# Hash attention and an MLP mixer on one core: wide hash products for the first pair, a new cadence of weight conversion, and an early fetch of the second turned batch

## The chip, the cores and the metric

The kernel runs on one core of one Trainium2 chip. The metric is the time of one execution on the device in microseconds (us), as the median of some runs. A run's time is about 1.8 us longer than the span of its instructions in the trace, so spans and times are not mixed below: a figure is called a span where it is one.

## The reference, cut to what matters

```python
# attention: batch 4, heads 8, sequence 768, head size 64, six hash bits
q_bits = (np.einsum('bhsd,dk->bhsk', q, proj) > 0)      # k_bits alike
mask = q_bucket[:, :, :, None] == k_bucket[:, :, None, :]
scores = np.where(mask, scale * q @ k^T, -1e9)
attn = softmax(scores);  x = attn @ v                   # -> (B, S, 512)
# mixer, weights in float64
h = relu(x^T @ w_tok1) @ w_tok2                         # token mixing
u = x + h^T
out = u + relu(u @ w_ch1) @ w_ch2                       # channel mixing
```

The kernel has three stages: attention for 16 pairs of heads (each in two halves of 384 queries), token mixing for four batches, and channel mixing. The weights come as float64; the chip turns each piece of 128x768 into float32 with five VectorE operations, a square on ScalarE, and a sixth VectorE operation. Below, such a piece is a *conversion*, and its three steps are *begin*, *join* and *end*. Attention leaves its result as XT, channels on partitions; token mixing wants batches 0 and 1 (and 2 and 3) *turned*, so XT goes out to memory in a *bounce* and comes back with *fetch*.

## The kernel before

The hash of a pair is four 32-wide products side by side. VectorE makes plus or minus a half of them, and a transfer brings the bits into the rows where they act as six extra channels of the score product (a seventh row carries a constant). For the first pair, nothing hides that transfer.

```python
def hashes(n):
    g = pool.tile([P, HALF], BF16, name="g", tag="g", bufs=2)
    ps = psum.tile([P, 2, 512], F32, name="hp", tag="sc", bufs=3)[:, 0]   # a bank of the scores
    for j in range(4):
        nc.tensor.matmul(ps[32 * j : 32 * j + 32, :HALF], projblk, loaded[n][0][:, j % 2, sl], ...)
    for rows in [slice(0, 64), slice(64, P)] if n == 0 else [slice(0, P)]:
        nc.vector.tensor_scalar(g[rows], ps[rows, :HALF], 0.0, 0.5, op0=ALU.is_gt, op1=ALU.subtract)
        ...                                     # n == 0: scaled on VectorE
    if n:
        nc.scalar.mul(g, g, bitscale)           # later pairs: scaled on ScalarE
    ...                                         # eight transfers g -> bit rows
```

One half of attention, in program order. `weights.some` does one third of a conversion in each half, so the square falls now into first, now into second halves:

```python
now = Half(n, half)
now.scores()                      # six chunks: product, bits' product, exponential
if half == 0: add_values(n)
now.add(0)
... quotients.sums()              # first halves: sums of the pair before
if half == 0 and n + 1 < len(pairs):
    hashes(n + 1); load_qk(n + 2)
if quotients: quotients.newton()  # three VectorE operations, four copies on ScalarE
if half and n and n % 2 == 0: bounce(pool, n - 2)
now.add(1)
if n:
    weights.some(third); third = (third + 1) % 3
if before: before.weigh()         # 12 products (24 records in a trace), then num on ScalarE
```

The end of attention and the start of token mixing:

```python
    before.weigh()
    quotients.divide()
    bounce(pool, len(pairs) - 2)  # last bounce: waits for VectorE's transposes
# token mixing
    fetch(1, x1)                  # same queue, behind it
    jobs = jobs(weights(pool))    # first loads of weights, behind that
    # jobs: three conversions of w_ch1 (two pieces), two jobs of weight sums, eight conversions of w_ch2;
    # mix1 and mix2 do one job after each of their parts
    for b in range(B):
        mix1(b)
        if b: mix2(b - 1)
    mix2(B - 1)
```

Of the kernel before, what the change touches and what calls it, by code (L numbers as in the profile page):

```python
# [36 lines left out]
F32 = mybir.dt.float32  # L37
# [11 lines left out]
def kernel(  # L49
# [40 lines left out]

    ident = const.tile([P, P], F32, name="ident")
    make_identity(nc, ident)
    ones = const.tile([P, D], F32, name="ones")
    nc.vector.memset(ones, 1.0)

    projblk = const.tile([P, 32], F32, name="projblk")
    nc.scalar.dma_start(out=projblk, in_=proj_pair)


    bitscale = const.tile([P, 1], F32, name="bitscale")  # L100
    nc.gpsimd.memset(bitscale, BIG)
    for j in range(4):
        if j % 2 == 0:
            nc.gpsimd.memset(bitscale[32 * j : 32 * j + 32], 1.0)
        else:
            for i in range(2):
                nc.gpsimd.affine_select(
                    out=bitscale, in_=bitscale, compare_op=ALU.not_equal, fill=-NB * BIG,
                    base=-(32 * j + 16 * i + NB), pattern=[[0, 1]], channel_multiplier=1,
                )  # L110
    largest = const.tile([P, B * NP], F32, name="largest")
# [14 lines left out]
    class Conversion:  # L126
# [72 lines left out]

        def some(self, k):  # L200

            (self.begin, self.join, self.end)[k]()
            if k == 0:
                self.fetch()

# [46 lines left out]
    def attention(pool, psum, W1, W2, x0):  # L252
        zeroed = [pool.tile([P, 2, S], BF16, name=f"bits{n}", tag=f"bits{n}", bufs=1) for n in range(2)]
        loaded = {}

        def load_qk(n):
            if n >= len(pairs):
                return
            b, hp = pairs[n]
            t = pool.tile([P, 2, S], F32, name="qk", tag="qk", bufs=3)  # L260
            for sl in [slice(0, HALF), slice(HALF, S)] if n == 0 else [slice(0, S)]:
                nc.sync.dma_start(out=t[:, :, sl], in_=qk[b, hp, :, :, sl])
            loaded[n] = [t, None, None, None]
# [18 lines left out]
        def hashes(n):  # L282

            g = pool.tile([P, HALF], BF16, name="g", tag="g", bufs=2)
            ps = psum.tile([P, 2, 512], F32, name="hp", tag="sc", bufs=3)[:, 0]
            for j in range(4):
                sl = slice(HALF * (j // 2), HALF * (j // 2) + HALF)
                nc.tensor.matmul(  # L288
                    ps[32 * j : 32 * j + 32, :HALF], projblk, loaded[n][0][:, j % 2, sl],
                    start=True, stop=True,  # L290
                )
            for rows in [slice(0, 64), slice(64, P)] if n == 0 else [slice(0, P)]:
                nc.vector.tensor_scalar(
                    g[rows], ps[rows, :HALF], 0.0, 0.5, op0=ALU.is_gt, op1=ALU.subtract,
                )
                if n == 0:
                    nc.vector.tensor_scalar(g[rows], g[rows], bitscale[rows], None, op0=ALU.mult)
            if n:
                nc.scalar.mul(g, g, bitscale)
            for j in range(4):  # L300
                sl = slice(HALF * (j // 2), HALF * (j // 2) + HALF)
                for i in range(2):
                    at = 32 * j + 16 * i
                    issuer = nc.scalar if n == 0 and i else nc.sync
                    issuer.dma_start(
                        out=zeroed[n % 2][D * i : D * i + NB + 1, j % 2, sl], in_=g[at : at + NB + 1],
                    )

        class Half:
# [5 lines left out]
            def scores(self):  # L315

                qkt, bits = loaded[self.n][0], zeroed[self.n % 2]
                qs = slice(HALF * self.half, HALF * self.half + HALF)
# [10 lines left out]
                def exponential(sc):  # L329
                    e = pool.tile([P, 2, HALF], F32, name="e", tag="e", bufs=12)  # L330
                    nc.scalar.activation(e, sc[:, :, :HALF], ACT.Exp, scale=SCALE)  # L331
                    self.es.append(e)

                waiting = []
                for c in range(NR):
                    sc = psum.tile([P, 2, 512], F32, name="sc", tag="sc", bufs=3)
                    product(sc, qkt, c, True)
                    if first and c < GR:
                        waiting.append((c, sc))
                        if c == GR - 1:  # L340
                            for c, sc in waiting:
                                product(sc, bits, c, False)
                            for c, sc in waiting:
                                exponential(sc)
                        continue
                    product(sc, bits, c, False)
                    exponential(sc)

            def add(self, k):
# [28 lines left out]
        class Quotients:  # L378
# [34 lines left out]
            def divide(self):  # L413
# [4 lines left out]
                )  # L418


        nc.scalar.preload_act_table_set("natural_log_exp_and_others")
        load_qk(0)
        for t in zeroed:
            nc.gpsimd.memset(t, 0.0)
        load_qk(1)

        idle = psum.tile([P, 512], F32, name="idle", tag="sm", bufs=1)
        for _ in range(14):
            nc.tensor.matmul(idle[:D, :D], ones, ones, start=True, stop=True)
        hashes(0)  # L430
        load_v(0)
        weights = Conversion(
            pool,
            [(w_tok1, W1, 3, (0, NR)), (w_tok2, W2, 1, (0, NJ)), (w_ch1, WC1, 1, (0, NCB - 1))],
            bufs=2,
        )
        before, both = None, []
        third = 0
        for n in range(len(pairs)):
            for half in range(2):  # L440
# [17 lines left out]
                now.add(1)  # L458
                if n:
                    weights.some(third)  # L460
                    third = (third + 1) % 3
                if before:
# [7 lines left out]
                before = now  # L470
        while third or weights.fetched:
            weights.some(third)
            third = (third + 1) % 3
        quotients = Quotients(both)
# [3 lines left out]
        quotients.divide()  # L478
        bounce(pool, len(pairs) - 2)

# [87 lines left out]
    def tokens(pool, psum, W1, W2, x0, weights, jobs, T):  # L568
# [7 lines left out]
        if not turned:  # L576
            fetch(1, x1)
        jobs = jobs(weights(pool)) if jobs else []

        def job():  # L580
            if jobs:
                jobs.pop(0)()
# [50 lines left out]
        mix2(B - 1)  # L633
        while jobs:
            job()
# [195 lines left out]
    def attention_and_tokens(W1, W2, x0):  # L831
# [7 lines left out]
        def weights(pool):  # L839
            return Conversion(  # L840
                pool, [(w_ch1, WC1, 1, (NCB - 1, NCB)), (w_ch2, WC2, 3, (0, NHT))], bufs=3,
            )

        def jobs(conversion):
            n1, n2 = DCH // NW, NHT * DM // NW
            return [
                *[conversion.one] * (n1 + 1),
                *weight_sums(
                    WC1, SW1, slice(0, NCB // 2), slice(NCB // 2, NCB),
                    slice(0, DCH // 2), slice(DCH // 2, DCH),  # L850
                ),
                *[conversion.one] * n2,
            ]
# [65 lines left out]
```

## Time and profile before

| What | Before |
|---|---|
| Median of the runs | 861.52 us (3 runs, 861.51 to 861.9) |
| The profiled run | 860.13 us, span 858.3 us, mean clock of TensorE 0.992 |
| TensorE busy | 842.5 us, 98% |

The stretches of the stages, from the profile of the kernel before. The columns are the stretch, its length, then busy time and number of instructions of TensorE, its weight loads, VectorE, ScalarE and GpSimd, TensorE's granted clock, the share of the transfer engines and GB/s. The stretches are attention from the first weighing, the last sums and weighing, and token mixing:

```profile
22.49:320.57 298.08, 298.08 (x2059) 136.87 (x2057) 246.05 (x300) 231.76 (x356) 0.00 (x0) 1.00 0.39 127
320.57:326.07 5.50, 5.50 (x34) 1.92 (x32) 3.11 (x5) 3.13 (x6) 0.00 (x0) 1.00 0.00 0
326.07:420.07 94.00, 87.27 (x225) 44.16 (x224) 74.91 (x100) 14.79 (x20) 0.00 (x0) 0.95 0.44 151
```

Of these three stretches, only token mixing has TensorE idle (94.00 against 87.27 us) and under a lower clock (0.95). Attention shows a full TensorE.

### The profile page before, as it was taken

Reading aid. Unit: us, or ns where it says so; the run is one execution under the profiler, and the core shown is the slowest. Engines: PE = TensorE matmul, PEld = TensorE weight load, DVE = VectorE, ACT = ScalarE, POOL = GpSimd, SP = SyncE. Lnnn points to the kernel's source line nnn. Section 1 sums busy time; section 2 is a strip of 40 time slices with the busy share of each in tenths; the row PEclk is TensorE's granted clock in tenths of the full one; section 3 lists DMA queues with packets and bytes.
Section 4 is the critical chain, followed back from the end, with each engine's and each line's share of the span. In section 5 each row is a group of like instructions: output and inputs, shape, how many; then the busy total and the mean of one; then the engine's idle time right before and its main releaser. Section 6 shows DMA issues by size and latency. Waiting matters only on the chain.

```text
span 858.3 us, 9068 instructions
## 1 busy us (share of the span) xinstructions
PE 842.5 (98%) x3449; PEld 386.3 (45%) x3449; DVE 530.8 (62%) x650; ACT 316.8 (37%) x492; POOL 52.8 (6%) x51
## 2 busy tenths in 40 slices
PE   8999999999999998999999999999999999999997
PEld 4444444444444443554544444444444444444444
DVE  3788878788888882999565383624467332336411
ACT  4777778778778772122011101011210101111000
POOL 1000000000000000000001112001110201011110
PEclk9999999999999999999999999999999999999999
DMA  4235353362534315632102101312210120000001
GB/s 151 88 145 173 105 166 114 113 204 97 150 113 129 134 38 188 234 129 75 37 0 74 73 1 61 112 72 73 74 37 29 36 94 13 0 0 1 24 25 52
DMA packets 48866, 73.72 MB, mean 86 GB/s; under 512 B 27952, under 2 KB 29616, under 8 KB 48816
## 3 DMA queue, kind: packets, MB, share of 16 engines
q1 hardware_dynamic: 48472, 72.90, 25.0%
q8 instruction: 29, 0.48, 0.2%
q14 instruction: 21, 0.17, 0.1%
q10 hardware_dynamic: 344, 0.17, 0.1%
HBM read 59.79 MB, written 12.58 MB: 84 GB/s over the span
## 4 chain that ended last, share of the span: by engine, by line
PE 88%; DVE 8%; DMA 2%; issue 1%; ACT 0%; SPq 0%; DVEq 0%; ACTq 0%
PE b L673 50%; PE sc L324 19%; PE acc L366 15%; PE sums L390 2%; PE t L617 1%; PE hp L288 1%; DVE tmp L184 1%; DVE tmp L168 1%; DMA raw<-in_moe_w_ch 1%; DVE XT L623 1%; DVE WC L195 1%; DVE tmp L180 1%; DVE tmp L165 1%; DVE tmp L185 1%; DMA qk<-in_qk 1%
## 5 line engine op out<-in xcount | busy, mean ns | idle before, releaser
L324 PE MATMUL sc<-qk 64*128 64x384 f32 x768 | 160.5, 497 | 1.0 <-ACT e L331 0.7
L331 ACT ACTIVATE e<-sc 128x768 f32<-128x768 f32 x192 | 151.3, 813 | 17.6 <-PE sc L324 17.1
L680 ACT COPY p<-b 128x512 f32<-128x512 f32 x72 | 42.3, 587 | 302.6 <-PE b L673 302.6
L366 PE MATMUL acc<-e,vn 128*64 128x384 f32 x768 | 130.9, 490 | 0.0
L358 DVE TENSOR_TENSOR esd<-esd,e 128x768 f32<-128x768 f32 x128 | 122.3, 955 | 10.0
L673 PE MATMUL b<-r,WC 128*128 128x512 f32 (+1 forms) x300 | 125.6, 575 | 0.0
L673 PE MATMUL b<-T,SW 128*128 128x512 f32 x216 | 96.6, 592 | 0.0
L324 PEld LDWEIGHTS sc<-qk 64*128 64x128 f32 x768 | 66.7, 188 | 58.3 <-issue 43.8
L673 PEld LDWEIGHTS b<-r,WC 128*128 128x128 f32 x300 | 57.0, 190 | 67.1 <-issue 63.6
L366 PEld LDWEIGHTS acc<-e,vn 128*64 128x64 f32 x768 | 52.3, 137 | 74.9 <-issue 74.9
L673 PE MATMUL b<-T,WC 128*128 128x512 f32 x144 | 67.7, 592 | 0.0
L703 DVE TENSOR_TENSOR r<-p,u 128x512 f32<-128x512 f32 x18 | 12.5, 693 | 86.5 <-ACT u L680 86.5
L673 PE MATMUL b<-XT,WC 128*128 128x512 f32 x144 | 64.7, 592 | 0.0
L324 PE MATMUL sc<-bits 64*128 64x384 bf16 x384 | 63.4, 324 | 1.3 <-DMA bits<-g 1.3
L673 PEld LDWEIGHTS b<-T,SW 128*128 128x128 f32 x216 | 41.0, 190 | 51.7 <-issue 50.9
L699 POOL TENSOR_TENSOR p<-p,p 128x512 f32<-128x512 f32 x18 | 22.8, 1264 | 652.2 <-ACT p L680 641.5
L673 PE MATMUL b<-r,SW 128*128 128x512 f32 x144 | 62.8, 592 | 0.0
L598 PE MATMUL t<-x,W 128*128 128x512 f32 x96 | 45.1, 629 | 3.8 <-DMA x<-bounced 3.8
L617 PE MATMUL t<-W,r 128*128 128x384 f32 x128 | 43.5, 499 | 2.9 <-DVE XT L623 2.9
L354 DVE SCALAR_TENSOR_TENSOR esd<-e 128x768 f32<-128x768 f32 x32 | 30.6, 956 | 21.8 <-ACT e L331 21.6
L680 ACT COPY u<-b 128x512 f32<-128x512 f32 x24 | 14.1, 587 | 79.1 <-PE b L673 79.1
L673 PEld LDWEIGHTS b<-T,WC 128*128 128x128 f32 x144 | 27.4, 190 | 34.4 <-issue 34.4
(79 smaller groups left out, 737.2 us busy)
## 6 DMA issues: line engine op xcount, KB each, us to landing
raw<-in_moe_w_ch SPq DMA_DIRECT2D x16, 768.0 KB
seen<-in_qk SPq DMA_DIRECT2D x16, 768.0 KB
qk<-in_qk SPq DMA_DIRECT2D x15, 768.0 KB
vn<-in_v SPq DMA_DIRECT2D x16, 384.0 KB
vt<-in_vT SPq DMA_DIRECT2D x16, 384.0 KB
bounced<-stage SPq DMA_DIRECT2D x32, 192.0 KB
x<-bounced SPq DMA_DIRECT2D x4, 1536.0 KB
out<-p SPq DMA_DIRECT2D x18, 256.0 KB
```

Of the source, the lines that this page charges most:

```text
L324: nc.tensor.matmul(sc[:, i, :HALF], t[rows, 1, P * c : P * c + P], t[rows, 0, qs], start=start, stop=not start,)
L331: nc.scalar.activation(e, sc[:, :, :HALF], ACT.Exp, scale=SCALE)
L354: nc.vector.scalar_tensor_tensor(self.d, es[0], NR * EPS, es[1], op0=ALU.add, op1=ALU.add,)
L358: nc.vector.tensor_tensor(self.d, self.d, e, op=ALU.add)
L366: nc.tensor.matmul(acc[D * i : D * i + D], vn[:, i, c], e[:, i], start=(c == 0), stop=(c == NR - 1),)
L390: nc.tensor.matmul(ps[at : at + 32], ones[:, :32], self.halves[h].d[:, i], start=True, stop=True,)
L598: nc.tensor.matmul(ps, W1[:, r, P * j : P * j + P], x[:, r], start=(r == 0), stop=(r == NR - 1),)
L617: nc.tensor.matmul(ps[:, :HALF], r1[:, j, P * cb : P * cb + P], W2[:, j, HALF * half : HALF * half + HALF], start=(j == 0), stop=(j == NJ ...
L673: nc.tensor.matmul(self.ps[i][:, cols], left(k), right(k)[:, cols], start=first and k == ks[0], stop=k == ks[-1], skip_group_check=True,)
L680: nc.scalar.copy(c, self.ps[i])
L699: nc.gpsimd.tensor_tensor(p7, p5, p7, op=ALU.add)
L703: nc.vector.tensor_tensor(r[:, 3], p7, u, op=ALU.add)
```

## The change

It has three parts. *Start:* the first pair's bits come from four 128-wide products whose result already stands in the right rows, so VectorE writes the bits and no transfer is needed. The first key/query load is split over two queues. *Cadence:* second halves do end, fetch and begin of a conversion, first halves the join; so twelve conversions fit into attention where ten did, and the last block of the first channel weight is among them. *Fetch:* the fetch of the second turned batch and the first loads of weights go ahead of the last bounce. The diff, cut to its core:

```diff
+        def turnover(self):
+            self.end()
+            self.fetch()
+            self.begin()
 ...
+                issuer = nc.scalar if n == 0 and sl.start else nc.sync
+                issuer.dma_start(out=t[:, :, sl], in_=qk[b, hp, :, :, sl])
 ...
+        def first_hashes(which, half):
+            sl = slice(HALF * half, HALF * half + HALF)
+            ps = psum.tile([P, 512], F32, name="hw", tag="sm" if which else "acc", bufs=1)[:, :HALF]
+            nc.tensor.matmul(ps, projwide, loaded[0][0][:, which, sl], start=True, stop=True)
+            to = bitrows[0][:, which, sl]
+            nc.vector.tensor_scalar(to, ps, 0.0, 0.5, op0=ALU.is_gt, op1=ALU.subtract)
+            if which:
+                nc.vector.tensor_scalar(to, to, widescale, None, op0=ALU.mult)
 ...                                          # in the first half's scores():
+                if first:
+                    first_hashes(0, 0)
+                    first_hashes(1, 0)
                 for c in range(NR):
 ...
                         if c == GR - 1:
+                            first_hashes(1, 1)
                             for c, sc in waiting:
                                 product(sc, bits, c, False)
 ...
+                if first:
+                    first_hashes(0, 1)
 ...
-        hashes(0)
-            [(w_tok1, W1, 3, (0, NR)), (w_tok2, W2, 1, (0, NJ)), (w_ch1, WC1, 1, (0, NCB - 1))],
+            [(w_tok1, W1, 3, (0, NR)), (w_tok2, W2, 1, (0, NJ)), (w_ch1, WC1, 1, (0, NCB))],
 ...
-                if n:
-                    weights.some(third)
-                    third = (third + 1) % 3
+                if half:
+                    weights.turnover()
+                else:
+                    weights.join()
 ...
         quotients.divide()
-        bounce(pool, len(pairs) - 2)
 ...
             fetch(1, x1)
-        jobs = jobs(weights(pool)) if jobs else []
+            jobs = jobs(weights(pool))
+            bounce(pool, len(pairs) - 2)
```

More of the change, by code (lines that the diff above doesn't have):

```diff
@@ L88, with cancel @@
     const = ctx.enter_context(tc.tile_pool(name="const", bufs=1))
-    ident = const.tile([P, P], F32, name="ident")
-    make_identity(nc, ident)
+    projs = const.tile([P, P + 32], F32, name="projs")
+    nc.scalar.dma_start(out=projs, in_=proj_pair)
+    projwide, projblk = projs[:, :P], projs[:, P:]
     ones = const.tile([P, D], F32, name="ones")
     nc.vector.memset(ones, 1.0)
-    projblk = const.tile([P, 32], F32, name="projblk")
-    nc.scalar.dma_start(out=projblk, in_=proj_pair)
+    def cancel(scale, at):
+        nc.gpsimd.affine_select(
+            out=scale, in_=scale, compare_op=ALU.not_equal, fill=-NB * BIG,
+            base=-at, pattern=[[0, 1]], channel_multiplier=1,
+        )
+    widescale = const.tile([P, 1], F32, name="widescale")
+    nc.gpsimd.memset(widescale, 0.0)
+    for i in range(2):
+        nc.gpsimd.memset(widescale[D * i : D * i + NB], BIG)
+        cancel(widescale, D * i + NB)
     bitscale = const.tile([P, 1], F32, name="bitscale")
@@ L106 @@
             for i in range(2):
-                nc.gpsimd.affine_select(
-                    out=bitscale, in_=bitscale, compare_op=ALU.not_equal, fill=-NB * BIG,
-                    base=-(32 * j + 16 * i + NB), pattern=[[0, 1]], channel_multiplier=1,
-                )
+                cancel(bitscale, 32 * j + 16 * i + NB)
+    ident = const.tile([P, P], F32, name="ident")
+    make_identity(nc, ident)
     largest = const.tile([P, B * NP], F32, name="largest")
@@ L198, in end @@
             )
-        def some(self, k):
-            (self.begin, self.join, self.end)[k]()
-            if k == 0:
-                self.fetch()
+        def turnover(self):
+            self.end()
+            self.fetch()
+            self.begin()
         def one(self):
@@ L252, in attention @@
     def attention(pool, psum, W1, W2, x0):
-        zeroed = [pool.tile([P, 2, S], BF16, name=f"bits{n}", tag=f"bits{n}", bufs=1) for n in range(2)]
+        bitrows = [pool.tile([P, 2, S], BF16, name=f"bits{n}", tag=f"bits{n}", bufs=1) for n in range(2)]
         loaded = {}
@@ L261, in load_qk @@
             for sl in [slice(0, HALF), slice(HALF, S)] if n == 0 else [slice(0, S)]:
-                nc.sync.dma_start(out=t[:, :, sl], in_=qk[b, hp, :, :, sl])
+                issuer = nc.scalar if n == 0 and sl.start else nc.sync
+                issuer.dma_start(out=t[:, :, sl], in_=qk[b, hp, :, :, sl])
             loaded[n] = [t, None, None, None]
@@ L291, in hashes @@
                 )
-            for rows in [slice(0, 64), slice(64, P)] if n == 0 else [slice(0, P)]:
-                nc.vector.tensor_scalar(
-                    g[rows], ps[rows, :HALF], 0.0, 0.5, op0=ALU.is_gt, op1=ALU.subtract,
-                )
-                if n == 0:
-                    nc.vector.tensor_scalar(g[rows], g[rows], bitscale[rows], None, op0=ALU.mult)
-            if n:
-                nc.scalar.mul(g, g, bitscale)
+            nc.vector.tensor_scalar(g, ps[:, :HALF], 0.0, 0.5, op0=ALU.is_gt, op1=ALU.subtract)
+            nc.scalar.mul(g, g, bitscale)
             for j in range(4):
@@ L303, in hashes @@
                     at = 32 * j + 16 * i
-                    issuer = nc.scalar if n == 0 and i else nc.sync
-                    issuer.dma_start(
-                        out=zeroed[n % 2][D * i : D * i + NB + 1, j % 2, sl], in_=g[at : at + NB + 1],
-                    )
+                    nc.sync.dma_start(
+                        out=bitrows[n % 2][D * i : D * i + NB + 1, j % 2, sl], in_=g[at : at + NB + 1],
+                    )
+        def first_hashes(which, half):
[6 more added lines that the diff above has]
+                nc.vector.tensor_scalar(to, to, widescale, None, op0=ALU.mult)
         class Half:
@@ L315, in scores @@
             def scores(self):
-                qkt, bits = loaded[self.n][0], zeroed[self.n % 2]
+                qkt, bits = loaded[self.n][0], bitrows[self.n % 2]
                 qs = slice(HALF * self.half, HALF * self.half + HALF)
@@ L418, in divide @@
                 )
+        load_qk(0)
         nc.scalar.preload_act_table_set("natural_log_exp_and_others")
-        load_qk(0)
-        for t in zeroed:
-            nc.gpsimd.memset(t, 0.0)
+        nc.gpsimd.memset(bitrows[1], 0.0)
         load_qk(1)
@@ L437, in attention @@
         before, both = None, []
-        third = 0
         for n in range(len(pairs)):
@@ L458, in attention @@
                 now.add(1)
-                if n:
-                    weights.some(third)
-                    third = (third + 1) % 3
+                if half:
+                    weights.turnover()
+                else:
+                    weights.join()
                 if before:
@@ L470, in attention @@
                 before = now
-        while third or weights.fetched:
-            weights.some(third)
-            third = (third + 1) % 3
+        assert not (weights.fetched or weights.begun or weights.ready)
         quotients = Quotients(both)
@@ L577, in tokens @@
             fetch(1, x1)
-        jobs = jobs(weights(pool)) if jobs else []
+            jobs = jobs(weights(pool))
+            bounce(pool, len(pairs) - 2)
         def job():
-            if jobs:
+            if not turned and jobs:
                 jobs.pop(0)()
@@ L633, in tokens @@
         mix2(B - 1)
-        while jobs:
+        while not turned and jobs:
             job()
@@ L839, in weights @@
         def weights(pool):
-            return Conversion(
-                pool, [(w_ch1, WC1, 1, (NCB - 1, NCB)), (w_ch2, WC2, 3, (0, NHT))], bufs=3,
-            )
+            return Conversion(pool, [(w_ch2, WC2, 3, (0, NHT))], bufs=3)
         def jobs(conversion):
-            n1, n2 = DCH // NW, NHT * DM // NW
             return [
-                *[conversion.one] * (n1 + 1),
                 *weight_sums(
@@ L851, in jobs @@
                 ),
-                *[conversion.one] * n2,
+                *[conversion.one] * (NHT * DM // NW + 1),
             ]
@@ L898 @@
         "in_proj": np.ascontiguousarray(inputs["proj"]),
-        "in_proj_pair": np.zeros((2 * D, 32), np.float32),
+        "in_proj_pair": np.zeros((2 * D, 2 * D + 32), np.float32),
     }
@@ L902 @@
         proj = inputs["proj"]
-        arrays["in_proj_pair"][D * i : D * i + D, 16 * i : 16 * i + proj.shape[1]] = proj
+        for at in (D * i, 2 * D + 16 * i):
+            arrays["in_proj_pair"][D * i : D * i + D, at : at + proj.shape[1]] = proj
     for name in _WEIGHTS:
```

## The prediction

> **What bounds the kernel now.** I read the page first, then the waits of TensorE, then the chain, then the timeline around each hole. On the page, line 1 is busy time by engine and the second line heads the chain that ended last:
>
> ```profile
> PE 842.5 (98%) x3449; PEld 386.3 (45%) x3449; DVE 530.8 (62%) x650; ACT 316.8 (37%) x492; POOL 52.8 (6%) x51
> ...
> PE 88%; DVE 8%; DMA 2%; issue 1%; ACT 0%; SPq 0%; DVEq 0%; ACTq 0%
> ```
>
> TensorE is the bound, so time can be won only where it is idle or runs slowly. The waits of TensorE (total, count, longest) list the holes:
>
> ```profile
> PE t L598 <- DMA x<-bounced: 3.8, 1, 3.8
> PE t L617 <- DVE XT L623: 2.9, 1, 2.9
> PE sc L324 <- DMA bits<-g: 1.3, 1, 1.3
> ```
>
> The timeline (start, length, engine) shows what each hole costs in all, by groups of the same work:
>
> ```profile
> 326.07 10.57 PE L598 MATMUL t<-x,W 128*128 128x512 f32 x24
> 329.95 2.18 SPq L232 DMA_DIRECT2D bounced<-stage  x4
> 332.24 0.58 SPq L239 DMA_DIRECT2D x<-bounced  x1
> 340.46 13.61 PE L598 MATMUL t<-x,W 128*128 128x512 f32 x24 [3.82 <-DMA x<-bounced]
> 374.52 10.48 PE L617 MATMUL t<-W,r 128*128 128x384 f32 x32
> 407.07 0.95 DVE L195 SCALAR_TENSOR_TENSOR WC<-raw,tmp 128x768 f32<-128x768 f32 x1
> 408.54 12.02 PE L617 MATMUL t<-W,r 128*128 128x384 f32 x32 [2.92 <-DVE XT L623]
> ```
>
> Hole 1: the second batch (x) is asked for at 332.24, because SyncE's queue stands behind four writes that wait for VectorE's transposes. Its product starts at 340.46 after 3.82 us idle, then takes 13.61 us where the same 24 records took 10.57. Hole 2: VectorE is still converting weights (L195) when it should empty PSUM (L623); 2.92 us idle, then 12.02 in place of 10.48.
>
> At the start, the chain and the timeline show the hash bits:
>
> ```profile
> 8.99 1.85 DMA bits<-g
> 11.77 0.82 ACT e L331
> ...
> 18.33 0.61 ACT L299 ACTIVATE g<-g,bitscale 128x384 bf16<-128x384 bf16 x1
> 18.84 4.60 ACT L331 ACTIVATE e<-sc 128x768 f32<-128x768 f32 x6
> 22.49 4.09 PE L366 MATMUL acc<-e,vn 128*64 128x384 f32 x24
> ```
>
> The first scores wait for a bounce through DMA until 10.97 and the first exponential runs at 11.77. But note L299 at 18.33: ScalarE scales the second pair's bits ahead of the second half's exponentials. A small loss repeats in attention, shown by two half-stages of equal work and what ScalarE did in the longer one:
>
> ```profile
> 46.14 5.05 PE sc L324 x36
> 56.64 5.28 PE sc L324 x36
> ...
> 57.11 0.91 ACT L194 ACTIVATE raw<-raw 128x768 f32<-128x768 f32 x1
> 58.37 4.43 ACT L331 ACTIVATE e<-sc 128x768 f32<-128x768 f32 x6
> ```
>
> **What the Trainium skill says.** (1) "TensorE: Matmul & The Clock Gate", Part 1: an idle window of about 3.4 us halves the clock until a busy window has passed. The trace agrees: weight loads follow each other every 0.86 us after hole 1 and every 0.43 us before it. (2) Same page, Part 3: products with few output columns run side by side in column tiles. Agrees: four 32-wide hash products take 0.65 us together in the chain, as one full-width product of 384 columns does (L617: 10.32/16 = 0.645). (3) Same page, "Architectural detail": ScalarE and VectorE are strict FIFO. Nothing in this trace contradicts it; my start estimate rests on it. (4) "DMA: Bandwidth & Descriptors", "Issuing engines are not separate DMA queues": transfers from different queues share the 16 engines and interleave. This trace has no large pair at once to show it.
>
> **The change, part by part.**
>
> *Fetch of the second batch.* Now issued before the last bounce, so SyncE no longer waits for the transposes at 329.95. Its buffer may still wait for TensorE's last use of the memory, at the latest the end of attention at 326.0. Before, issue to start of the product took 340.46 - 332.24 = 8.2 us, so the data is there by 334.3 at the latest, ahead of 336.6 when it is wanted. Removed: 3.82 idle and 13.61 - 10.47 = 3.14 of slow clock, **6.96 us**.
>
> *First channel weight converted in attention.* VectorE's token stage had 10 conversions and has 8. One conversion is 0.60+0.99+0.60+0.99+0.96+0.87 = 5.0 us by its starts in the timeline, and the first need no longer wait for weights landing at 342.5. In before's clock, VectorE does transposes to 329.95, the weight sums (four of 1.7) to 336.9, two conversions to 346.0, and the emptying of the first mix2 from 348 to 359, with a conversion between. By the built order the last heavy conversion then ends near 388, and the emptying of the third mix2, whose first bank is full near 389, is prompt. Mix2 of the last batch (starting 398) finds free banks. Removed: 2.92 + (12.02 - 10.48), **4.46 us**. Check of both: with no hole the stage is 4 x (10.30 + 10.32) = 82.5 us where it took 420.07 - 326.07 = 94.0; difference 11.5.
>
> *Attention's cadence.* A conversion per 2 halves in place of 3. Does VectorE still fit? In the pair from 124.86 to 144.42 (19.56 us), which has a bounce, a join and an end, VectorE idled 0.25 + 0.76 + 0.59 = 1.60 us. The change adds a begin, 0.60 + 0.99 = 1.59 us: it just fits. It makes the adds of the next half 1.3 us later, which the two waits for the hash and for the reciprocal swallow; sums wait for nothing new. So hidden. Two gains follow. The square (L194) now always stands in second halves, away from the reciprocal copies, so the five halves of 5.28 become 5.05: 5 x 0.23 = **1.2 us**. And the last pair has no conversion (join, 2.5 us before its adds), so the last sums, 1.52 in the chain where others take 0.78, no longer wait: **0.7 us**.
>
> *Start.* Removed: the bits' transfers (1.85) and two of four small VectorE steps. Added: four full-width products of 0.64 in place of 0.65 together, so 1.9 us more TensorE work. The queue half-and-half load lets the key/query halves and the next pair share the engines; I take the first half at TensorE at 5.1 in place of 4.64 (an estimate; the next transfer is 0.39 MB beside it). Two products, partly at the slow clock, to 6.7; three scores of 0.65 to 8.6; third product 9.25; first exponential near **9.6**, 2.2 earlier. But that gain doesn't reach the second half. The fourth product follows the sixth score chunk, which waits for the third exponential: 9.6 + 2.4 + 0.1 + 0.8 + 0.64 = 13.55. VectorE has its bits (0.56) ahead of the three adds (3.0) and then the next pair's hash (0.6); ScalarE's L299 (0.6) waits for that, and the next six exponentials stand behind it in FIFO: 13.55 + 0.2 + 0.56 + 3.0 + 0.6 + 0.6 = **18.5**, where before it was 18.84. TensorE meanwhile has three chunks to do (to 16.7) and idles till 19.4. If the clock stays fast, weighing starts 0.6 earlier than 22.49; if the 2.7 us hole drops the clock, 1.1 later. About evens: **0.2 us lost**, give or take 1.2.
>
> Sum: 6.96 + 4.46 + 1.2 + 0.7 - 0.2 = 13.1, so 861.5 - 13.1 = **848.4 us**.
>
> **The rivals.** *A: the start gains fully*, 2 to 2.5 us, 846. For: the first exponential really is earlier. Against: VectorE and ScalarE orders as built. *B: VectorE becomes attention's bound.* Its margin on a pair with a bounce is 0.01 us by the above; 0.3 us short on each of five such pairs would give 850, and spread over twelve pairs 852. Against: pairs without a bounce have 1.8 us to spare, so a lag should not add up. *C: hole 2 stays*, since one conversion more (5 us) stands between TensorE's banks and their emptying at mix2(1): 852 to 853. Against: eight banks and a lead of over 10 us by my walk through the order. *D: the fetch is held* by memory still in use or by sharing with the two weight loads behind it (0.79 MB each beside 1.57 MB): a remnant of hole 1 of 1 to 3 us, 850 to 851. Before, such loads also stood right behind it.
>
> **Range and chances.** The token stage is firm to about 0.7 us, attention to about 1, the start to about 1.5; together some 2, with a tail to the slow side from B to D. 845.8 to 851.0 holds 8 in 10. Faster by over 2% needs 844.3, 4 us better than the sum: even rival A in full falls short. Slower by over 2% has no mechanism.
>
> **What would show it.** In the changed profile: no wait for x and none for XT L641 (L623 before) among TensorE's waits; mix1 of the second batch about 10.5 long right after the first; the sc groups all 5.05; sums last 0.8; first exponential near 9.6 but the second half's six near 18.5, behind a g scale, with a hole in TensorE of some 2.7 us before it. Wrong if the second half's exponentials start near 16, if sc or acc groups of the first twelve pairs stretch, or if a new wait stands in the token stage.

## The result, and the profile after

The changed kernel took **846.46 us** (median of 4 runs, 845.84 to 846.74) where the kernel before took 861.51 us in the same comparison (4 runs, 859.83 to 861.9). The ratio is 0.983, with an interval of 0.981 to 0.985: 1.7% less time, within 2%. Ratios here are the mean time of one kernel's fast runs over that of the other's fast runs of the same rounds, so they are not quite the ratio of the quoted medians.

Lines were added above most of the code, so a line number moves: the scores L324 are now L340, weighing L366 is L388, the sums L390 are L412, the products of token mixing L598 and L617 are L616 and L635, and the emptying L623 is L641. From the page of the changed kernel, busy time by engine and the head of the chain:

```profile
PE 835.2 (99%) x3449; PEld 384.8 (46%) x3449; DVE 532.3 (63%) x652; ACT 318.7 (38%) x492; POOL 52.0 (6%) x55
...
PE 98%; DVE 1%; DMA 0%; ACT 0%; issue 0%; DVEq 0%; ACTq 0%
```

TensorE's share of the chain went from 88% to 98%, VectorE's from 8% to 1%. TensorE's waits in the changed kernel:

```profile
PE sc L340 <- DVE g L305: 1.5, 1, 1.5
...
PE sc L340 <- ACT e L347: 0.9, 2, 0.6
PE hw L319 <- DMA qk<-in_qk: 0.8, 1, 0.8
```

Both large waits of token mixing are gone, and one new wait of 1.5 us on the hash g stands at the head. The same three stretches as before, in the changed kernel:

```profile
22.24:319.13 296.89, 296.89 (x2058) 137.17 (x2057) 256.95 (x314) 235.92 (x358) 0.00 (x0) 1.00 0.43 136
319.13:323.93 4.80, 4.80 (x34) 1.79 (x32) 1.58 (x3) 3.12 (x6) 0.00 (x0) 1.00 0.87 330
323.93:406.52 82.59, 82.59 (x227) 42.67 (x226) 66.17 (x88) 12.88 (x18) 0.00 (x0) 1.00 0.39 124
```

Token mixing has TensorE busy all of its 82.59 us at a full clock. Subtracting stage by stage gives the account of the whole gain in the traces:

| Stage | Before | After | Gain | Predicted |
|---|---|---|---|---|
| Start, to the first weighing | 22.49 | 22.24 | 0.25 | -0.2 |
| Attention | 298.08 | 296.89 | 1.19 | 1.2 |
| Last sums and weighing | 5.50 | 4.80 | 0.70 | 0.7 |
| Token mixing | 94.00 | 82.59 | 11.41 | 11.42 |
| Channel mixing | 438.23 | 438.28 | -0.05 | 0 |
| Span | 858.30 | 844.80 | 13.50 | 13.1 |

In the timeline of the changed kernel (start, length, engine) the fetch is issued before the last weighing ends, mix1 of the first and second batch run as one group, and the four bounce writes stand behind:

```profile
315.21 0.38 SPq L251 DMA_DIRECT2D x<-bounced  x1
...
323.93 20.87 PE L616 MATMUL t<-x,W 128*128 128x512 f32 x48
...
327.81 3.16 SPq L244 DMA_DIRECT2D bounced<-stage  x4
```

In its chain a score group, and the last sums that took 1.52 us before:

```profile
36.83 5.05 PE sc L340 x36
...
319.20 0.78 PE sums L412 x8
```

In the chain all groups of 36 score records are 5.04 or 5.05, except the very last half's 5.15. At the start, from the timeline (the number in brackets is the idle time before, and what ended it):

```profile
9.70 4.43 ACT L347 ACTIVATE e<-sc 128x768 f32<-128x768 f32 x6 [6.58 <-PE sc L340]
...
17.60 0.55 DVE L305 TENSOR_SCALAR g<-hp 128x384 bf16<-128x384 f32 x1
...
18.21 0.92 PE L340 MATMUL sc<-qk 64*128 64x384 f32 x4 [1.51 <-DVE g L305]
18.25 0.62 ACT L306 ACTIVATE g<-g,bitscale 128x384 bf16<-128x384 bf16 x1 [3.30 <-DVE g L305]
18.77 4.41 ACT L347 ACTIVATE e<-sc 128x768 f32<-128x768 f32 x6
```

The first exponential is 2 us earlier than before, the second half's are where they were: 18.77 against 18.84. This is the one place where the change gains nothing of what it could.

### The profile page after: what moved, and what is told of

It reads as the page before. It is cut to its first block, busy times and chain, and to the rows that moved or that the text cites. A ratio compares the mean times of both kernels' runs of the same rounds, so it can differ in the third digit from the quotient of the medians.

```text
span 844.8 us, 9068 instructions
## 1 busy us (share of the span) xinstructions
PE 835.2 (99%) x3449; PEld 384.8 (46%) x3449; DVE 532.3 (63%) x652; ACT 318.7 (38%) x492; POOL 52.0 (6%) x55
## 4 chain that ended last, share of the span: by engine, by line
PE 98%; DVE 1%; DMA 0%; ACT 0%; issue 0%; DVEq 0%; ACTq 0%
PE b L691 51%; PE sc L340 19%; PE acc L388 15%; PE t L616 5%; PE t L635 5%; PE sums L412 1%; PE hp L301 1%; DMA qk<-in_qk 0%; PE hw L319 0%; DVE esd L380 0%; ACT e L347 0%; DVE esd L376 0%; ACT g L306 0%; DVE bits L321 0%; DVE u L777 0%
## 5 line engine op out<-in xcount | busy, mean ns | idle before, releaser
L340 PE MATMUL sc<-qk 64*128 64x384 f32 x768 | 158.6, 492 | 2.4 <-DVE g L305 1.5
L347 ACT ACTIVATE e<-sc 128x768 f32<-128x768 f32 x192 | 152.9, 812 | 14.0 <-PE sc L340 13.2
L388 PE MATMUL acc<-e,vn 128*64 128x384 f32 x768 | 130.9, 490 | 0.0
L380 DVE TENSOR_TENSOR esd<-esd,e 128x768 f32<-128x768 f32 x128 | 122.3, 955 | 10.3 <-ACT e L347 0.5
L340 PEld LDWEIGHTS sc<-qk 64*128 64x128 f32 x768 | 66.5, 187 | 58.1 <-issue 44.9
L388 PEld LDWEIGHTS acc<-e,vn 128*64 128x64 f32 x768 | 52.3, 137 | 74.9 <-issue 74.3
L340 PE MATMUL sc<-bits 64*128 64x384 bf16 x384 | 62.9, 323 | 0.0
L691 PEld LDWEIGHTS b<-r,SW 128*128 128x128 f32 x144 | 27.4, 190 | 34.4 <-issue 34.0
L691 PEld LDWEIGHTS b<-XT,WC 128*128 128x128 f32 x144 | 27.3, 190 | 34.1 <-issue 33.8
L616 PE MATMUL t<-x,W 128*128 128x512 f32 x96 | 41.8, 593 | 0.0
```

What stands on the lines that cost most here:

```text
L340: nc.tensor.matmul(sc[:, i, :HALF], t[rows, 1, P * c : P * c + P], t[rows, 0, qs], start=start, stop=not start,)
L347: nc.scalar.activation(e, sc[:, :, :HALF], ACT.Exp, scale=SCALE)
L380: nc.vector.tensor_tensor(self.d, self.d, e, op=ALU.add)
L388: nc.tensor.matmul(acc[D * i : D * i + D], vn[:, i, c], e[:, i], start=(c == 0), stop=(c == NR - 1),)
L616: nc.tensor.matmul(ps, W1[:, r, P * j : P * j + P], x[:, r], start=(r == 0), stop=(r == NR - 1),)
L691: nc.tensor.matmul(self.ps[i][:, cols], left(k), right(k)[:, cols], start=first and k == ks[0], stop=k == ks[-1], skip_group_check=True,)
```

## The experiments

Twelve runs were made, in four calls. The first four and the next three ran on one chip, the two calls after that on two others. The kernel before: 858.82 us (9 runs), 859.98 (11 runs), 860.98 (one run) and 860.25 (9 runs). Every kernel gave the reference's result.

**Theory at this point.** The sum of the prediction is right because TensorE is the bound and every idle or slow stretch of it was removed. But how the 11.4 us divide between fetch and conversions was only argued: 6.96 and 4.46. *Rival:* the early fetch, by taking the weights' loads along, does nearly all of it.

### 1. The changed kernel once more

No edit.

> The changed kernel again, as the yardstick of this chip: 846.5 us, and no wait for the x fetch or the bank emptying in the token stage. The runs of the kernel before beside it tell whether 1.5 us of the change's gain is clock: the theory that slow clock windows of 1.7 us each come or go in the kernel before expects its runs to differ by such steps with their granted clock, and the changed kernel's not to; the rival, that the time outside the profiled span differs, expects time less span to differ between the two kernels.

Measured: 845.87 us (5 runs, 845.71 to 847.44), ratio 0.985 (0.983 to 0.987). On this chip the kernel before took 858.82 us. The difference of medians is 12.95 us here and was 15.05 in the first comparison. The changed kernel moved by 0.6 us; the kernel before by 2.7. The theory holds in the main: the nine spans of the kernel before go from 856.3 us (clock 0.995) to 859.6 (0.991), and time less span is 1.8 to 1.9 us for both kernels, which speaks against the rival. But one run of the changed kernel moved too (span 845.6, clock 0.998, where the others have 843.8 to 844.3 at 1.0).

### 2. The last bounce back ahead of the fetch

```diff
         quotients.divide()
+        bounce(pool, len(pairs) - 2)
 ...
             jobs = jobs(weights(pool))
-            bounce(pool, len(pairs) - 2)
```

> The last bounce again ahead of the fetch of the second batch, all else as changed. Theory (the fetch alone makes the first hole): TensorE waits about 3.8 us for x and then runs at the slow clock for one or two windows, +5.5 to +7 us over the changed kernel, 852 to 853.5 us, with no wait for the bank emptying. Rival (the holes hang together: weights that arrive late put VectorE late as well): the second wait comes back too, +9 to +11 us.

Measured: 856.18 us (4 runs, 854.69 to 857.31), ratio 0.997. Slower than the theory expected: 10.3 us over the changed kernel's median, the size that the rival named, but the second wait that the rival went by isn't in the trace. The second batch's product in this kernel's timeline:

```profile
339.97 13.39 PE L616 MATMUL t<-x,W 128*128 128x512 f32 x24 [5.56 <-DMA x<-bounced]
```

Hole 1 is back and larger than before, 5.56 us in place of 3.82. The product starts at 339.97, almost where it did before (340.46), but TensorE got there at 334.4 in place of 336.6, since the rest of the change made attention shorter. A gain ahead of a hole that ends on a transfer is lost in the hole. Hole 2 isn't there. Token mixing takes 415.08 - 323.84 = 91.24 us, 8.65 more than with the early fetch: 5.56 idle, 13.39 - 10.46 = 2.93 slow, and 0.16 of seams. The profiled run was the fastest of the four (span 852.9 us, the others 853.9 to 855.5), so what those lost on top isn't seen.

### 3. The last block of the first channel weight back in token mixing

```diff
-            [..., (w_ch1, WC1, 1, (0, NCB))],
+            [..., (w_ch1, WC1, 1, (0, NCB - 1))],
 ...
-            return Conversion(pool, [(w_ch2, WC2, 3, (0, NHT))], bufs=3)
+            return Conversion(pool, [(w_ch1, WC1, 1, (NCB - 1, NCB)), (w_ch2, WC2, 3, (0, NHT))], bufs=3)
 ...                                     # and its three jobs ahead of the weight sums
```

> The last block of the first channel weight again converted in the token stage, fetch still early. My prediction's sum (the move is worth the whole second hole): +4.5 us, 851 us. Rival (the early fetch also brings the weights 17 us earlier, so VectorE needs the move only for its last microsecond): by walking the order, the emptying of the third mix2 begins near 396.7 where TensorE wants the bank at 396.2, a wait of 1 us or less and no slow clock: +1 us, 847.5 us.

Measured: 849.27 us (4 runs, 847.62 to 850.06), ratio 0.989. By the time alone this looks like 3.4 us more than the changed kernel, between the two expectations. The trace doesn't say so. Its hole 2, from the timeline:

```profile
396.93 10.59 PE L635 MATMUL t<-W,r 128*128 128x384 f32 x32 [0.80 <-DVE XT L641]
```

The hole is 0.80 us and doesn't slow the clock; token mixing takes 407.35 - 323.71 = 83.64 us, 1.05 more than in the changed kernel. The runs of this one kernel spread over 2.4 us, so two more looks at the same kernel were taken on another chip, and one at the kernel before.

> The late conversion again, for its trace: its five runs before spread over 2.4 us of span at the same granted clock. Theory (VectorE reaches the bank emptying within a microsecond of TensorE wanting it, so any slip of a weight's landing comes out in full): where the span is longer than 845.8, the wait for the bank emptying in the third and fourth mix2 is longer by as much, up to 3.2 us. Rival: that wait stays at 0.8 us and the time is lost at the start.

> As the run before it: a second chance of a trace with a longer span. Same expectations.

> The kernel before once more, for its trace. Theory (its spread of 3.6 us in span is slow clock windows of 3.4 us, each costing up to 1.7): a span that differs from 858.3 comes with fewer or more slow windows at the start, at the x fetch or at the bank emptying, while the idle times there stay 1.3, 3.8 and 2.9 us. Rival: the waits themselves differ.

Measured: 847.14 and 849.05 us, spans 845.4 and 847.3, both with the same 0.78 us at hole 2 and 83.63 and 83.64 us of token mixing. So the rival holds: the difference of 1.9 us lies at the start. The first two hash products in the second look, and then in the third:

```profile
4.96 1.53 PE L319 MATMUL hw<-qk,projs 128*128 128x384 f32 x4 [0.88 <-DMA qk<-in_qk]
```

```profile
4.80 2.90 PE L319 MATMUL hw<-qk,projs 128*128 128x384 f32 x4 [0.55 <-DMA qk<-in_qk]
```

In the third look these four records took 1.37 us longer, and the first twelve score records behind them 2.75 us where they took 2.21: together 1.9 us. By the clock records, TensorE's clock came to full speed at 8.77 us of the span there, and at 3.74 us in the second look. So the part of the conversions is 1.05 us when the early fetch is there; what these two looks differ by is the start's. That the slower runs of the first chip were late starts too is inferred from their spans; only the fastest of those was profiled, and why three of four should start late isn't shown. The look at the kernel before gave 861.19 us (span 859.4) with waits of 3.6 us at hole 1 and 4.0 at hole 2 where the first profile had 3.8 and 2.9: it varies by about a microsecond in the holes themselves, so the waits do differ, as the rival of that look had it.

### 4. The early fetch alone, in the kernel before

This closes the square: with and without fetch, with and without the conversions moved.

```diff
         quotients.divide()
-        bounce(pool, len(pairs) - 2)
 ...
             fetch(1, x1)
-        jobs = jobs(weights(pool)) if jobs else []
+            jobs = jobs(weights(pool))
+            bounce(pool, len(pairs) - 2)
```

> The kernel before with the early fetch of the second turned batch alone (the last bounce moved behind the fetch and the first weights). The prediction's split (fetch 6.96, conversions 4.46) says about 7 us less than the kernel before of the same rounds, 852 to 854 us. The theory from the undone parts (the early fetch also brings the mixers' weights earlier, so it takes most of the second hole with it) says 8.7 to 10.4 us less, about 849 us, with a wait of mix2's emptying of some 0.8 us left.

Measured: 849.2 us (4 runs, 848.9 to 849.36), ratio 0.987 (0.985 to 0.989); the kernel before took 860.25 in these rounds. That is 11.05 us less, where the prediction's split gives 7. What is left of hole 2, among TensorE's waits, and the stretch of token mixing:

```profile
PE t L617 <- DVE XT L623: 0.8, 1, 0.8
```

```profile
325.57:409.18 83.61, 82.85 (x226) 42.58 (x225) 75.11 (x100) 14.52 (x20) 0.00 (x0) 1.00 0.45 142
```

Token mixing fell by 94.00 - 83.61 = 10.39 us with not one conversion moved out of it; the other 0.8 of the 11.2 us between the spans lies mostly in the start and in channel mixing (0.4 and 0.3). Why hole 2 went too is told by the first conversion on VectorE, in the kernel before and then here:

```profile
342.53 0.56 DVE L165 TENSOR_SCALAR tmp<-raw 128x768 uint32<-128x768 uint32 x1 [12.61 <-DMA raw<-in_moe_w_ch]
```

```profile
329.33 0.52 DVE L165 TENSOR_SCALAR tmp<-raw 128x768 uint32<-128x768 uint32 x1
```

In the kernel before VectorE stood idle for 12.61 us waiting for the weights, whose loads were queued behind the fetch, which was behind the bounce. Here it begins 13.2 us earlier, and is that much less behind when the banks have to be emptied. The square, in us of token mixing:

| | Conversions as before | Conversions moved |
|---|---|---|
| Late fetch | 94.00 (before) | 91.24 (run 2) |
| Early fetch | 83.61 (this run); 83.64 (run 3) | 82.59 (changed kernel) |

The two kernels in the lower left cell differ in start and cadence and agree. Those of the upper row differ in both as well, which made hole 1 longer in run 2. The fetch is worth 10.39 us if it comes first and 8.65 if last; the conversions 2.76 or about 1.0. The rival of the theory holds, the prediction's split does not.

### 5. The start of the kernel before, the rest as changed

The edit puts back the narrow hash, its transfers, and the order of the constants and first loads, and leaves fetch and cadence.

```diff
-                if first:
-                    first_hashes(0, 0)
-                    first_hashes(1, 0)
 ...                                     # and the other two calls
+        hashes(0)
 ...
```

> The first pair's hash bits again by four narrow products and eight small transfers, with the loads, constants and queues of before; the token stage as changed. Theory (ScalarE's and VectorE's orders give the earlier exponentials back before the second half): +0.3 us when the clock is fast, up to +2 where the old start still falls to the slow clock, 846.8 to 848. Rival (the first exponential's 2.1 us carry through): +2 us or more in every run, 848.6.

Measured: 846.54 us (5 runs, 846.22 to 847.28), ratio 0.985 (0.984 to 0.987), against 845.87 for the changed kernel on this chip. The start part of the change is worth about 0.7 us, and the intervals overlap, so it isn't told from nothing; the rival's 2 us or more did not come. The rest carries the gain.

### 6. The fourth hash product earlier

If the second half's exponentials are what keeps the start from gaining, then the order of work causes it: the fourth product follows the sixth chunk, and its bits, three adds and the next pair's hash queue up on VectorE. Here the fourth product follows the third.

```diff
                                 product(sc, bits, c, False)
+                            first_hashes(0, 1)
                             for c, sc in waiting:
 ...
-                if first:
-                    first_hashes(0, 1)
```

> The fourth wide product moved from after the sixth score chunk to right behind the first three chunks' bits, into TensorE's 0.58 us hole. Theory (VectorE waits for that product with its adds, the next pair's hash waits for the adds, ScalarE's scale for the hash and the second half's exponentials for the scale): the chain loses its 3 us, the second half's first exponential comes near 15.7 in place of 18.8, weighing starts near 19.2 in place of 22.3, -3 us, 843.4 us. Rival (these exponentials wait for something else): nothing gained, 846.5 us.

Measured: **843.67 us** (5 runs, 843.29 to 844.03), ratio 0.981 (0.980 to 0.983). The second half's exponentials and the first weighing in this kernel's timeline:

```profile
15.50 4.60 ACT L347 ACTIVATE e<-sc 128x768 f32<-128x768 f32 x6
...
19.15 4.09 PE L387 MATMUL acc<-e,vn 128*64 128x384 f32 x24
```

Weighing starts at 19.15 in place of 22.24 (22.02 in the trace of run 1), and TensorE waits for nothing after the first load. This version beats both kernels; its highest run is below the lowest of the changed kernel, 845.71 on this chip. Whether it is over 2% faster than the kernel before stays unclear, since the interval begins at 0.980.

### 7. The second pair's scale on VectorE

Is it ScalarE, whose exponentials stand behind the g scale, or VectorE, which comes late to the hash?

```diff
-            nc.scalar.mul(g, g, bitscale)
+            if n == 1:
+                nc.vector.tensor_scalar(g, g, bitscale, None, op0=ALU.mult)
+            else:
+                nc.scalar.mul(g, g, bitscale)
```

> The second pair's hash bits scaled on VectorE in place of ScalarE, the fourth product late as in the changed kernel. Theory A, as my prediction had it (ScalarE's FIFO alone holds the second half): its exponentials start near 15.6 and weighing begins near 19.5, -2.8 us, 843.7 us. Theory B (TensorE's third chunk waits for VectorE's hash as well, since the hash product took one of the three score banks: 1.5 us idle at 18.2 in the changed trace): exponentials of two chunks run early, but the third chunk still starts at 18.2, -0.7 us, 845.8 us.

Measured: 846.88 us (5 runs, 844.91 to 847.32), ratio 0.985. The five runs fall into two groups, spans near 843.2 and near 845.3, as late and early starts do, so the median tells nothing; the lower group is about 0.8 us below the changed kernel's usual spans of 843.8 to 844.3. In the trace (span 843.2) the exponentials begin at 16.34, and weighing at 21.24, 1.0 us earlier than in the changed kernel but 2.1 later than in run 6. But the first load was late in this trace: its first hash product stands at 5.29 us, where the changed kernel has 4.89 and run 6 has 4.83. Counted from there, weighing comes 1.4 us earlier than in the changed kernel and 1.6 later than in run 6. So the scale's place in ScalarE's queue is about half; the other half goes with the fourth product's late place, and this run doesn't split it further. The detail expected of the third chunk was wrong: it was the fourth that waited 0.34 us for g.

### 8. The halves swapped

The cadence puts the square into second halves. To test that this is what frees the score groups, turnover goes into first halves and join into second.

```diff
                 if half:
-                    weights.turnover()
-                else:
                     weights.join()
+                else:
+                    weights.turnover()
```

> Turnover (with the square) in first halves and join in second, the other way round than in the changed kernel. Theory (a square that stands behind the reciprocal copies on ScalarE delays the second half's first exponential): each of the 11 or 12 second halves after a square takes 5.28 in place of 5.05, +2.6 to 2.9 us, 849.3 us. Rival (the 5.28 of before came from VectorE's begin in the same half): no half is longer, 846.5 us.

Measured: 853.07 us (6 runs, 852.11 to 854.95), ratio 0.992: worse than expected by 3.8 us. In the profiled run (span 853.2) ScalarE in a first half, with the copies of the reciprocal and the square ahead of the second half's exponentials:

```profile
39.00 2.07 ACT L433 COPY rec<-rec 32x384 f32<-32x384 f32 x4 [0.71 <-DVE rec L427]
41.09 0.89 ACT L206 ACTIVATE raw<-raw 128x768 f32<-128x768 f32 x1
...
42.35 4.42 ACT L347 ACTIVATE e<-sc 128x768 f32<-128x768 f32 x6
```

TensorE waits here 1.40 us for a bank of the scores. From one weighing to the next over a second half took 9.30 us, 0.23 over the undisturbed 9.07, in every other pair, and 9.62 in the pairs that come right after a bounce's transposes; with the first of the twelve, 10.74 (the wait of 1.40 us is in it), this makes 5.8 us in all. The mechanism is confirmed with the same 0.23 us; its size was underestimated, because after a bounce VectorE also reaches the reciprocal later, and the copies shift with it (they begin 2.77 us after the weighing before them, in place of 2.46). The profiled run also had two losses of its own: the 1.40 us above, once, as the second pair's values had come late behind a load of weights, and a late clock at the start (2.90 us for the first hash products).

### 9. Two idle products more

Idle products warm TensorE's clock before the first load. Would a longer run of them end the late starts? The edit is on the version of run 6.

```diff
-        for _ in range(14):
+        for _ in range(16):
```

> The version with the early fourth product, with 16 instead of 14 idle products ahead of the first load. Theory: some of the spread between the runs of the changed kernels comes from TensorE's clock warming one stretch of 3.4 us later at the start; with the idle products reaching nearer to the first load fewer runs start late, so the spread stays within 1 us and the median is 843.7 or less. Rival: the idle products have no part in it: the same 843.7 and the same spread, or 0.1 to 0.3 us more.

Measured: 843.52 us (5 runs, 843.46 to 843.71), ratio 0.981. The spread is 0.25 us where it was 0.74, the median 0.15 less, but on another chip, and run 6 had no late start in its five runs either. Inconclusive: a late start is too rare for five runs to tell.

## Why the prediction was right or wrong

- **The bound.** Right. TensorE was the bound, and the time won is the time that it was idle or slow; its busy share went to 99%.
- **Token mixing without a hole, 82.5 us.** Right: 82.59.
- **Fetch, 6.96 us, and conversions, 4.46 us.** The sum is right, the attribution failed. The sum did not need the attribution: both holes went, whichever part closed them. "The first need no longer wait for weights landing at 342.5" stands in the prediction under the conversions. It belongs to the fetch, since the weights' loads stand behind it in the queue: runs 2, 3 and 4 give the fetch 8.65 to 10.39 and the conversions 1.0 to 2.76. The low 2.76 has hole 1 in it too, which grew by 1.74 us as the work ahead of it got shorter: 2.76 + 1.74 is 4.5, so the prediction's figure for hole 2 was sound where the fetch stays late.
- **Cadence, 1.2 us.** Right: 1.19 in the stretch of attention, and run 8 found the 0.23 us per half again by moving the square back. The lag of 1.3 us behind a bounce came (in the pair from 124.14, the next half's first add stands 1.26 us later than in the pair before), and it was swallowed by VectorE's two waits: its idle 0.76 us before g fell to none, its 0.59 before t to 0.19. Rival B, which made VectorE the bound, did not come.
- **Last sums, 0.7 us.** Right: 0.70 in the stretch.
- **Start, 0.2 us lost.** First exponential 9.6, found 9.70; second half's exponentials 18.5, found 18.77. One step failed: the hole of 2.7 us. The prediction had TensorE do three chunks and then idle; but the next pair's hash product takes one of the three score banks, so the third chunk had itself to wait for g (1.51 us), and a further 0.33 us came behind it. The clock stayed full, and the start gained 0.25 us between the two profiles. That is within the spread: over all traces the first weighing stands at 22.06 to 23.40 us with the old start, and with the new one at 22.01 to 22.31 us, or 24.07 and 24.60 in two late starts (runs 6, 7 and 9, which moved other work there, left out). That the late second half is what holds the start is shown by run 6, which moved one call and gained 3.1 us at the first weighing (2.9 against run 1) and 2.2 in the median.
- **The subtraction, 861.5 - 13.1.** This is the largest term of the difference of 1.9 us. The holes were read in a run of 860.13 us, and their sum was taken from a median of 861.5. From the run in which they were read it gives 847.0, which leaves 0.5 us, about what the start came out better than its step. The kernel before itself varied between 858.05 and 861.9 us, with its holes and its clock; the changed kernel has no hole for that to vary in.

What is left open: which of the queued transfers held the second batch in run 2, where 9.0 us passed from issue to product and in the kernel before 8.2; and whether more idle products reduce late starts.

## What to carry to other kernels

A transfer that stands behind a waiting one in the same queue delays everything behind it: look not only for the load that the bound waits for but for all that was queued after it, and expect two holes that share such a queue to share their cure, so that gains undone one at a time do not add up to the gain together. Work ahead of a hole that ends on a transfer can't be won until the hole is gone. And take a sum that was read in one run from that run's time, not from another run's or a median.

## What the Trainium skill lacked or had wrong

- "TensorE: Matmul & The Clock Gate", Part 1, ties the slow clock to a whole idle window of about 3.4 us; only its section on a second failure mode says, without a number, that frequent short idles can do it too. In the kernel before TensorE was busy in part: by the clock records a slow stretch began at 12.10 us, and in the 3.41 us before it TensorE worked 1.87 us and its longest wait was 1.33 us. The next four score records of one chunk took 1.65 us where they take 0.81. A hole of 2.92 us slowed it as well; in other places 1.51 + 0.33 us, or one hole of 0.8, did not. How much work in a window keeps the clock is stated nowhere. These runs bracket it: cut into stretches of 3.41 us at the edges of the clock records, the fourteen traces have nine stretches at full clock with 1.87 us of work or less, each followed by a slow one, and none with 1.90 us or more that is (busy time as the profile models it).
- Same page: the length of the slow stretch after a hole. By the clock records of the traces it was 6.83 us after hole 1 (3.8 us idle) in one run of the kernel before and 3.41 us after the same hole (3.6 us) in another. The page says that the window runs freely, that the warm-up varies from run to run, and that its cost is under 1% of a span. That holds here (1.9 us of a span of 847.3 is 0.2%), but it lacks the warning that follows: this is more than the start part of the change is worth, so five runs of one kernel fall into two groups. The mean granted clock doesn't show which: it was 0.999 in both looks of run 3.
- "DMA: Bandwidth & Descriptors", "Issuing engines are not separate DMA queues": what the page says of two engines' loads is not contradicted (the first load split over two queues reached TensorE at 4.65 to 5.29 us over the traces, at 4.48 to 4.80 on one queue). The section says that a second issuing engine saves only the time of issue. It leaves out the case that mattered here, and the page's anatomy of a DMA says only that a wait is made on the issuing sequencer, not what that does to the transfers behind it: a transfer that waits for VectorE holds the later, independent ones of the same queue, and with the order changed the first conversion began 13.2 us earlier (342.53 to 329.33, of which the shorter stages before account for 0.5).
